# Where the row statistics, the bias load and the last MLP product stand in a kernel of linear attention and MLP

## The chip, the cores and the metric

The kernel runs on one core of a Trainium2 chip. The metric is device time in microseconds of one execution, as the median of several runs. A profile describes one execution of the same kernel. TensorE is written PE (its weight loads PEld), VectorE DVE, ScalarE ACT, GpSimd POOL, SyncE SP.

## What is computed

For 2048 tokens of width 512, a layer norm feeds two branches that are added to the input: a linear attention with 32 heads of 16 (feature map: softmax of a projection and of its negative), and an MLP of width 1792 with the mish activation.

```python
def _A_ref(x, wqkv, w_phi, wo):
    # q, k, v: (x @ wqkv) split into 32 heads of 16
    pq = jnp.einsum("bhsd,hdf->bhsf", q, w_phi)
    pk = jnp.einsum("bhsd,hdf->bhsf", k, w_phi)
    phi_q = jnp.concatenate([_softmax(pq, axis=-1), _softmax(-pq, axis=-1)], axis=-1)
    phi_k = jnp.concatenate([_softmax(pk, axis=-1), _softmax(-pk, axis=-1)], axis=-1)
    kv = jnp.einsum("bhsf,bhsd->bhfd", phi_k, v)
    z  = jnp.einsum("bhsf->bhf", phi_k)
    num = jnp.einsum("bhqf,bhfd->bhqd", phi_q, kv)
    den = jnp.einsum("bhqf,bhf->bhq", phi_q, z)[..., None] + 1e-6
    o = num / den
    return (o, heads joined) @ wo

def _B_ref(x, w1, b1, w2):
    h = jnp.einsum("bsd,df->bsf", x, w1) + b1
    sp = jnp.log1p(jnp.exp(-jnp.abs(h))) + jnp.where(h > 0, h, jnp.zeros_like(h))
    act = h * jnp.tanh(sp)
    return jnp.einsum("bsf,fd->bsd", act, w2)

x = A_x
xn = _layernorm(x, axis=-1)
return x + _A_ref(xn, A_wqkv, A_w_phi, A_wo) + _B_ref(xn, B_w1, B_b1, B_w2)
```

## The kernel before

The tokens are worked on in four groups (NG) of 512, each of four tiles (TPG) of 128 rows. At the start all weights are loaded, w_phi is folded into the q and k weights (wqp, wkp), and the mean and the reciprocal deviation of every row are worked out: those of group 0 from one load, those of the other 12 tiles from a second one. A framework puts each engine's instructions in an order of its own, by priority and dependence, and derives the waits; a line's place in the text is not its place in the queue.

```python
xs_v = x2.rearrange("(g t p) d -> p (g t) d", t=TPG, p=P)
x_stats0 = prep_w.tile([P, TPG, D], BF16, name="x_stats0")
nc.sync.dma_start(x_stats0[:], xs_v[:, 0:TPG, :])
wqk = prep_w.tile([P, KT, 2 * D], BF16, name="wqk")
nc.scalar.dma_start(wqk[:], wqkv_v[:, :, 0 : 2 * D])
# ... (cut): w_phi on ACT, wv on SP, w1 on ACT, wo on SP, w2 on ACT
b1b = wts.tile([P, FT], BF16, name="b1b")
with nc.allow_non_contiguous_dma(reason="tiny bias load"):
    nc.scalar.dma_start(b1b[:], b1_v[:, :])
b1f = wts.tile([P, FT], FP32, name="b1f")
nc.vector.tensor_copy(b1f[:], b1b[:])
# ... (cut): tiles that live throughout
stats0 = prep_w.tile([P, TPG, nc.vector.BN_STATS_DIM], FP32, name="stats0")
for tt in range(TPG):
    nc.vector.bn_stats(stats0[:, tt, :], x_stats0[:, tt, :])
for tt in range(TPG):
    nc.vector.bn_aggr(mv[:, tt, :], stats0[:, tt, :])
nc.scalar.activation(rstd[:, 0:TPG], mv[:, 0:TPG, 1], ACT.Sqrt, bias=eps_t[:])
nc.vector.reciprocal(rstd[:, 0:TPG], rstd[:, 0:TPG])

def finish_ln_stats():
    statpool = tc.alloc_tile_pool(name="statpool", bufs=1)
    x_stats = statpool.tile([P, NT - TPG, D], BF16, name="x_stats")
    nc.sync.dma_start(x_stats[:], xs_v[:, TPG:NT, :])
    stats = statpool.tile([P, NT, nc.vector.BN_STATS_DIM], FP32, name="stats")
    for tt in range(TPG, NT):
        nc.vector.bn_stats(stats[:, tt, :], x_stats[:, tt - TPG, :])
    for tt in range(TPG, NT):
        nc.vector.bn_aggr(mv[:, tt, :], stats[:, tt, :])
    nc.scalar.activation(rstd[:, TPG:NT], mv[:, TPG:NT, 1], ACT.Sqrt, bias=eps_t[:])
    nc.vector.reciprocal(rstd[:, TPG:NT], rstd[:, TPG:NT])
    statpool.release()
# ... (cut): masks, and Wbd, the block diagonal of w_phi
    for mi, base_col in ((0, 0), (1, D)):
        pfs = [
            ps_fold.tile([P, D], FP32, name=f"pfold{mi}_{kt}", tag="fold")
            for kt in range(KT)
        ]
        for j in range(4):
            ptr = ps_prep.tile([P, D], BF16, name="ptrw", tag="prep")
            for kt in range(KT):
                nc.tensor.transpose(
                    ptr[:, kt * P : (kt + 1) * P],
                    wqk[:, kt, base_col + j * P : base_col + (j + 1) * P],
                    ident[:],
                )
            wT = tmp.tile([P, D], BF16, name="wT")
            nc.scalar.copy(wT[:], ptr[:])
            for kt in range(KT):
                nc.tensor.matmul(
                    pfs[kt][:, j * P : (j + 1) * P],
                    lhsT=wT[:, kt * P : (kt + 1) * P],
                    rhs=Wbd[:, j, :],
                    start=True,
                    stop=True,
                )
        dst = wqp if mi == 0 else wkp
        for kt in range(KT):
            nc.vector.tensor_copy(dst[:, kt, :], pfs[kt][:])
prep_w.release()
```

Pass A, for each group: normalise and transpose x, project to v, k and q, take both exponentials (stage_front); softmax sums and scaling (stage_phi); transposes of phi(q) and the sums over tokens kvacc (stage_kq); the first MLP product with exp (stage_h); ln and tanh over all 1792 units (stage_lt); the second MLP product (stage_mb), which runs one group late.

```python
# ... (cut): pools of pass A; PSUM: tr 1, kq 1 (two banks), mm 2, kv 1, oB 2
def stage_front(g):
    xg = xpool.tile([P, TPG, D], BF16, name="xg")
    nc.sync.dma_start(xg[:], x_g[g])
    # ... (cut): xn <- (xg - mean) * rstd, four tiles on DVE; xnT <- transposes of xn; for four tiles: pv -> vext, ppkq -> e1, e2 (exp of it and of its negative)

def stage_h(st):
    uu = mpool.tile([P, FT, 512], BF16, name="uu")
    for f in range(FT):
        ph = ps_mm.tile([P, 512], FP32, name="pmm", tag="mm")
        for kt in range(KT):
            nc.tensor.matmul(
                ph[:],
                lhsT=w1_sb[:, kt, f * P : (f + 1) * P],
                rhs=xnT[:, kt, :],
                start=(kt == 0),
                stop=(kt == KT - 1),
            )
        nc.scalar.activation(
            uu[:, f, :], ph[:], ACT.Exp, bias=b1f[:, f : f + 1]
        )
    return uu

def stage_lt(uu):
    th = mpool.tile([P, FT, 512], BF16, name="th", bufs=1)
    nc.scalar.activation(th[:], uu[:], ACT.Ln, bias=1.0)
    nc.scalar.activation(uu[:], uu[:], ACT.Ln)
    nc.scalar.activation(th[:], th[:], ACT.Tanh)
    return (uu, th)

def stage_mb(st, lt):
    lnu, th = lt
    acts = []
    for f in range(FT):
        a = apool.tile([P, 512], BF16, name="act")
        nc.vector.tensor_tensor(
            out=a[:], in0=lnu[:, f, :], in1=th[:, f, :], op=ALU.mult
        )
        acts.append(a)
    pobs = []
    for t in range(TPG):
        poB = ps_oB.tile([P, 512], FP32, name="poB", tag="oB")
        for f in range(FT):
            nc.tensor.matmul(
                poB[:],
                lhsT=acts[f][:, t * P : (t + 1) * P],
                rhs=w2_sb[:, f, :],
                start=(f == 0),
                stop=(f == FT - 1),
            )
        tt = g * TPG + t
        nc.vector.tensor_copy(xb_all[:, tt, :], poB[:])
    return pobs

st = [None] * NG
lt = [None] * NG
st[0] = stage_front(0)
finish_ln_stats()
for g in range(NG):
    uu = stage_h(st[g])
    if g > 0:
        stage_mb(st[g - 1], lt[g - 1])
    lt[g] = stage_lt(uu)
    stage_phi(st[g])
    stage_kq(st[g])
    if g + 1 < NG:
        st[g + 1] = stage_front(g + 1)
nc.vector.tensor_tensor(
    out=kvm[:],
    in0=kvacc[:],
    in1=KVmask[:, None, :].to_broadcast([P, 8, 136]),
    op=ALU.mult,
)
stage_mb(st[NG - 1], lt[NG - 1])
```

Pass B needs the sums over all tokens (kvm), so it runs after the last group: numerator and denominator from phi(q) (pnd), the quotient o_t, its transpose oT, then the output projection poA, started with an identity product that adds x, and the MLP result xb_all added at the end.

```python
# ... (cut): pools of pass B: o_t 5, oT 2, rdt 4, yg 2, xg2 2; PSUM: pnd 4, ptr2 2, poA 2

xbpool = p2.enter_context(tc.tile_pool(name="pb_x", bufs=2))
for g in range(NG):
    gs = slice(g * 512, (g + 1) * 512)
    xg2 = xbpool.tile([P, TPG, D], BF16, name="xg2")
    nc.scalar.dma_start(xg2[:], x_g[g])

    o_tiles = []
    for t in range(TPG):
        tok0 = g * 512 + t * P
        o_t = opool.tile([P, 512], BF16, name="o_t")
        for j in range(4):
            pnd = ps_w.tile([P, 136], FP32, name="pnd", tag="pnd")
            for pl in range(2):
                s = 2 * j + pl
                nc.tensor.matmul(
                    pnd[:],
                    lhsT=phiqT_all[:, s, tok0 : tok0 + P],
                    rhs=kvm[:, s, :],
                    start=(pl == 0),
                    stop=(pl == 1),
                )
            rdt = rpool.tile([P, 8], FP32, name="rdt")
            nc.vector.reciprocal(rdt[:], pnd[:, 128:136])
            nc.vector.tensor_tensor(
                out=o_t[:, j * P : (j + 1) * P].rearrange(
                    "p (h e) -> p h e", e=16
                ),
                in0=pnd[:, 0:128].rearrange("p (h e) -> p h e", e=16),
                in1=rdt[:, :, None].to_broadcast([P, 8, 16]),
                op=ALU.mult,
            )
        o_tiles.append(o_t)
    oT = oTpool.tile([P, 4, 512], BF16, name="oT")
    for j in range(4):
        ptr = ps_tr2.tile([P, 512], BF16, name="ptr2", tag="tr2")
        for t in range(TPG):
            nc.tensor.transpose(
                ptr[:, t * P : (t + 1) * P],
                o_tiles[t][:, j * P : (j + 1) * P],
                ident[:],
            )
        nc.scalar.copy(oT[:, j, :], ptr[:])

    yg = ypool.tile([P, TPG, D], BF16, name="yg")
    for t in range(TPG):
        tt = g * TPG + t
        poA = ps_oA.tile([P, 512], FP32, name="poA", tag="oA")
        nc.tensor.matmul(
            poA[:],
            lhsT=ident[:],
            rhs=xg2[:, t, :],
            start=True,
            stop=False,
        )
        for j in range(4):
            nc.tensor.matmul(
                poA[:],
                lhsT=oT[:, j, t * P : (t + 1) * P],
                rhs=wo_sb[:, j, :],
                start=False,
                stop=(j == 3),
            )
        nc.vector.tensor_tensor(
            out=yg[:, t, :], in0=poA[:], in1=xb_all[:, tt, :], op=ALU.add
        )
    nc.sync.dma_start(out_g[g], yg[:])
```

The softmax here doesn't subtract the row's maximum and nothing guards it: scores larger than these inputs give would overflow.

## Time and profile before

| what | value |
|---|---|
| time, median of 4 runs | 283.81 us (282.29 to 284.76) |
| span of the profiled run | 282.3 us, 3341 instructions |
| PE busy | 215.8 us (76%), 1277 matmuls |
| DVE busy | 198.0 us (70%), 504 instructions |
| ACT busy | 167.0 us (59%), 136 instructions |
| POOL busy | 2.1 us (1%) |
| DMA | 14.38 MB |

Busy time is the sum of the instructions of an engine. Matmuls overlap in the array, so a busy PE is not PE at its peak: one 128x512 matmul is listed with a mean of about 380 ns, and in a run of them one starts every 216 ns. The profile has, among others, a table of busy time by stretch of the span, groups of instructions by line and shape, a timeline, a list of who waited for whom, and a chain: from the last instruction back, at each step to what released it. In lines of the profile, L392 is line 392 of the kernel before; names such as `poB` are those of the tiles, and `out<-in` gives what an instruction writes and reads. Group 0 to 3 are the token groups.

### The profile page before, as it was taken

How to read it: one execution, taken by the hardware profiler on the slowest of the kernel's cores; microseconds unless marked ns; L12 is line 12 of the kernel's file. 1: busy time of each engine (PE TensorE's matmuls, PEld its weight loads, DVE VectorE, ACT ScalarE, POOL GpSimd, SP SyncE). 2: the span in 40 equal slices, each digit the busy share in tenths (PEclk: the TensorE clock that was granted, in tenths of full speed). 3: DMA queues.
4: the chain of work that ended last, by engine and by line, in shares of the span. 5: the costliest groups of instructions: out<-in, count | busy, mean ns of one | idle time of the engine just before them, and what ended most of it. 6: DMA issues, size and time to landing. Idle time of an engine off the chain costs nothing.

```text
span 282.3 us, 3341 instructions
## 1 busy us (share of the span) xinstructions
PE 215.8 (76%) x1277; PEld 109.1 (39%) x1298; DVE 198.0 (70%) x504; ACT 167.0 (59%) x136; POOL 2.1 (1%) x14
## 2 busy tenths in 40 slices
PE   1122238998784699986999996899997589889973
PEld 0122214443541244445444445444444434444531
DVE  0405954999762799836899946699965783788762
ACT  0040110777999587899887899868799900320330
POOL 2000000000000000000000000000000000000000
PEclk9999999999999599999999999999999979999998
DMA  6996022200002000000000000000000300043122
GB/s 229 371 354 163 0 74 78 74 0 0 2 0 74 0 1 2 1 0 2 0 0 0 2 0 0 2 0 1 0 2 0 130 21 0 0 152 112 39 74 74
DMA packets 14687, 14.38 MB, mean 51 GB/s; under 512 B 2640, under 2 KB 13648, under 8 KB 14672
## 3 DMA queue, kind: packets, MB, share of 16 engines
q1 hardware_dynamic: 7360, 7.34, 8.2%
q10 hardware_dynamic: 7312, 6.84, 7.6%
q8 instruction: 10, 0.16, 0.2%
q14 instruction: 5, 0.04, 0.0%
HBM read 12.08 MB, written 2.10 MB: 50 GB/s over the span
## 4 chain that ended last, share of the span: by engine, by line
PE 52%; ACT 18%; DVE 13%; DMA 8%; issue 7%; SPq 1%; ACTq 0%; DVEq 0%
PE poB L392 13%; PE pmm L359 13%; DMA x_stats<-in_A_x_dram 8%; PE ppkq L249 5%; PE ppkq L257 5%; PE poA L490 5%; ACT th L373 4%; ACT th L375 4%; PE pmm L237 4%; DVE stats L125 3%; ACT e L266 3%; DVE o_t L458 2%; DVE phiqT_all L330 2%; ACT e L267 2%; PE ptr L325 2%
## 5 line engine op out<-in xcount | busy, mean ns | idle before, releaser
L392 PE MATMUL poB<-w_sb,act 128*128 128x512 bf16 x218 | 52.0, 388 | 7.5 <-DVE act L384 7.1
L359 PE MATMUL pmm<-xnT,w_sb 128*128 128x512 bf16 x219 | 52.1, 378 | 1.1 <-ACT uu L366 0.8
L366 ACT ACTIVATE uu<-pmm,b1f 128x512 bf16<-128x512 f32 x56 | 37.2, 691 | 11.8 <-PE pmm L359 7.6
L392 PEld LDWEIGHTS <-act 128*128 128x128 bf16 x224 | 22.3, 100 | 35.1 <-DVE act L384 9.3
L359 PEld LDWEIGHTS <-w_sb 128*128 128x128 bf16 x224 | 21.8, 97 | 28.9 <-issue 4.7
L476 ACT COPY oT<-ptr 128x512 bf16<-128x512 bf16 x16 | 8.7, 588 | 39.3 <-PE ptr L471 22.5
L400 DVE CAST xb_all<-poB 128x512 bf16<-128x512 f32 x16 | 11.0, 690 | 21.1 <-PE poB L392 21.1
L384 DVE TENSOR_TENSOR act<-uu,th 128x512 bf16<-128x512 bf16 x56 | 19.6, 416 | 7.9 <-ACT th L375 7.9
L374 ACT ACTIVATE uu<-uu 128x7168 bf16<-128x7168 bf16 x4 | 24.7, 6177 | 0.1
L375 ACT ACTIVATE th<-th 128x7168 bf16<-128x7168 bf16 x4 | 24.7, 6177 | 0.0
L373 ACT ACTIVATE th<-uu 128x7168 bf16<-128x7168 bf16 x4 | 24.7, 6177 | 0.0
L266 ACT ACTIVATE e<-ppkq 128x1024 bf16<-128x1024 f32 x16 | 16.3, 1021 | 12.1 <-PE ppkq L257 12.0
L237 PE MATMUL pmm<-wv,xnT 128*128 128x512 bf16 x64 | 20.4, 400 | 0.2
L178 PE MATMUL pfold<-Wbd,wT 128*128 128x128 bf16 x32 | 4.9, 305 | 19.7 <-DVE wqp L187 10.6
L278 DVE TENSOR_REDUCE ss<-e 128x64 f32<-128x1024 bf16 x16 | 19.3, 1209 | 0.0
L284 DVE TENSOR_REDUCE ss<-e 128x64 f32<-128x1024 bf16 x16 | 19.3, 1206 | 0.0
L325 PE MATMUL ptr<-ident,e 128*128 128x128 bf16 x128 | 12.7, 217 | 8.3 <-DVE phiqT_all L330 8.2
L249 PE MATMUL ppkq<-wkp,xnT 128*128 128x512 bf16 x58 | 18.1, 403 | 1.2 <-ACT e L267 0.8
L330 DVE COPY phiqT_all<-ptr 128x512 bf16<-128x512 bf16 x32 | 13.6, 424 | 7.1 <-PE ptr L325 6.9
L257 PE MATMUL ppkq<-wqp,xnT 128*128 128x512 bf16 x64 | 17.3, 395 | 0.0
L497 DVE TENSOR_TENSOR yg<-poA,xb_all 128x512 bf16<-128x512 f32 x16 | 10.7, 689 | 8.9 <-PE poA L490 8.7
L449 PE MATMUL pnd<-kvm,phiqT_all 128*128 128x136 bf16 x128 | 14.1, 227 | 3.7 <-DVE kvm L416 1.9
(66 smaller groups left out, 289.4 us busy)
## 6 DMA issues: line engine op xcount, KB each, us to landing
w_sb<-in_B_w_dram ACTq DMA_DIRECT2D x2, 1792.0 KB, 18.8
xg<-in_A_x_dram SPq DMA_DIRECT2D x4, 512.0 KB, 3.5
xg<-in_A_x_dram ACTq DMA_DIRECT2D x4, 512.0 KB, 4.0
out_dram<-yg SPq DMA_DIRECT2D x4, 512.0 KB, 3.2
x_stats<-in_A_x_dram SPq DMA_DIRECT2D x1, 1536.0 KB, 21.8
wqk<-in_A_wqkv_dram ACTq DMA_DIRECT2D x1, 1024.0 KB, 7.6
x_stats<-in_A_x_dram SPq DMA_DIRECT2D x1, 512.0 KB, 6.1
wv<-in_A_wqkv_dram SPq DMA_DIRECT2D x1, 512.0 KB, 8.3
```

Source lines behind the costliest of these rows:

```text
L237: nc.tensor.matmul(pv[:], lhsT=xnT[:, kt, tok0 : tok0 + P], rhs=wv[:, kt, :], start=(kt == 0), stop=(kt == KT - 1),)
L249: nc.tensor.matmul(ppkq[:, 0, :], lhsT=xnT[:, kt, tok0 : tok0 + P], rhs=wkp[:, kt, :], start=(kt == 0), stop=(kt == KT - 1),)
L257: nc.tensor.matmul(ppkq[:, 1, :], lhsT=xnT[:, kt, tok0 : tok0 + P], rhs=wqp[:, kt, :], start=(kt == 0), stop=(kt == KT - 1),)
L266: nc.scalar.activation(e1[:], ppkq[:], ACT.Exp)
L278: nc.vector.reduce_sum(ss1[:], e1[:].rearrange("p s (h e) -> p s h e", e=16), axis=AX.X,)
L359: nc.tensor.matmul(ph[:], lhsT=w1_sb[:, kt, f * P : (f + 1) * P], rhs=xnT[:, kt, :], start=(kt == 0), stop=(kt == KT - 1),)
L366: nc.scalar.activation(uu[:, f, :], ph[:], ACT.Exp, bias=b1f[:, f : f + 1])
L373: nc.scalar.activation(th[:], uu[:], ACT.Ln, bias=1.0)
L374: nc.scalar.activation(uu[:], uu[:], ACT.Ln)
L375: nc.scalar.activation(th[:], th[:], ACT.Tanh)
L384: nc.vector.tensor_tensor(out=a[:], in0=lnu[:, f, :], in1=th[:, f, :], op=ALU.mult)
L392: nc.tensor.matmul(poB[:], lhsT=acts[f][:, t * P : (t + 1) * P], rhs=w2_sb[:, f, :], start=(f == 0), stop=(f == FT - 1),)
```

## The change

It changes four things. First, the rows of group 0 are loaded once, by POOL's queue, and both its statistics and its normalisation use that tile; the load kept apart for the statistics goes. Second, the statistics of the other 12 tiles, and the cast of the bias, are put behind the last vext copy of group 0 (`issue_after`), so that the weight folding and group 0 need not wait for them; the bias load moves from ACT's queue to SP's. Third, the pools of pass A are released one by one, so that those of pass B can be opened while the buffers of the MLP live on; the second MLP product of the last group is split into its element products (`mb_acts`) and its matmuls (`mb_mm`), and the matmuls may be put between the pieces of pass B. Fourth, in pass B the numerator tile holds two blocks, so that one reciprocal and one product serve both; PSUM buffers become 3 (pnd), 1 (transposes) and 2 (poA) beside 2 of the MLP; the quotient tiles have 8 buffers instead of 5, and x is loaded by POOL's queue.

```diff
@@ -80,8 +80,6 @@
 
     prep_w = tc.alloc_tile_pool(name="prep_w", bufs=1)
     xs_v = x2.rearrange("(g t p) d -> p (g t) d", t=TPG, p=P)
-    x_stats0 = prep_w.tile([P, TPG, D], BF16, name="x_stats0")
-    nc.sync.dma_start(x_stats0[:], xs_v[:, 0:TPG, :])
     wqk = prep_w.tile([P, KT, 2 * D], BF16, name="wqk")
     nc.scalar.dma_start(wqk[:], wqkv_v[:, :, 0 : 2 * D])
     Wsrc = prep_w.tile([P, 4, DH], BF16, name="Wsrc")
@@ -97,9 +95,8 @@
     nc.scalar.dma_start(w2_sb[:], w2_v[:, :, :])
     b1b = wts.tile([P, FT], BF16, name="b1b")
     with nc.allow_non_contiguous_dma(reason="tiny bias load"):
-        nc.scalar.dma_start(b1b[:], b1_v[:, :])
+        nc.sync.dma_start(b1b[:], b1_v[:, :])
     b1f = wts.tile([P, FT], FP32, name="b1f")
-    nc.vector.tensor_copy(b1f[:], b1b[:])
 
     phiqT_all = persist.tile([P, 8, S], BF16, name="phiqT_all")
     kvacc = persist.tile([P, 8, 136], FP32, name="kvacc")
@@ -107,14 +104,6 @@
     rstd = persist.tile([P, NT], FP32, name="rstd")
-    ... (cut: statistics of group 0, as printed above)
 
     def finish_ln_stats():
         statpool = tc.alloc_tile_pool(name="statpool", bufs=1)
@@ -187,24 +176,27 @@
                 nc.vector.tensor_copy(dst[:, kt, :], pfs[kt][:])
     prep_w.release()
 
-    with ExitStack() as p1:
-        ... (cut: pools as before)
-        def stage_front(g):
-            xg = xpool.tile([P, TPG, D], BF16, name="xg")
-            nc.sync.dma_start(xg[:], x_g[g])
+    if True:
+        mpool = tc.alloc_tile_pool(name="pa_mish", bufs=1)
+        apool = tc.alloc_tile_pool(name="pa_act", bufs=14)
+        ps_oB = tc.alloc_tile_pool(name="ps_oB", bufs=2, space=bass.MemoryType.PSUM)
+        ... (cut: the other pools of pass A, with their sizes as before, ps_kv last)
+
+        last_front = [None]
+
+        def stage_front(g, xg=None):
+            if xg is None:
+                xg = xpool.tile([P, TPG, D], BF16, name="xg")
+                nc.sync.dma_start(xg[:], x_g[g])
             xn = xnpool.tile([P, TPG, D], BF16, name="xn")
             for t in range(TPG):
                 tt = g * TPG + t
@@ -241,7 +233,7 @@
                         start=(kt == 0),
                         stop=(kt == KT - 1),
                     )
-                nc.vector.tensor_copy(
+                last_front[0] = nc.vector.tensor_copy(
                     vext[:, t, :, 0:128], pv[:].rearrange("p (j c) -> p j c", j=4)
                 )
                 ppkq = ps_kq.tile([P, 2, 512], FP32, name="ppkq", tag="pkq")
@@ -375,8 +367,7 @@
             nc.scalar.activation(th[:], th[:], ACT.Tanh)
             return (uu, th)
 
-        def stage_mb(st, lt):
-            g, xg, xnT, vext, e1_tiles, e2_tiles = st
+        def mb_acts(st, lt):
             lnu, th = lt
             acts = []
             for f in range(FT):
@@ -385,6 +376,10 @@
                     out=a[:], in0=lnu[:, f, :], in1=th[:, f, :], op=ALU.mult
                 )
                 acts.append(a)
+            return acts
+
+        def mb_mm(st, acts):
+            g = st[0]
             ...
@@ -400,10 +395,113 @@
                 nc.vector.tensor_copy(xb_all[:, tt, :], poB[:])
             return pobs
 
+        def stage_mb(st, lt):
+            return mb_mm(st, mb_acts(st, lt))
+
+        def alloc_passB_pools():
+            pb = {}
+            pb["x"] = tc.alloc_tile_pool(name="pb_x", bufs=2)
+            pb["ot"] = tc.alloc_tile_pool(name="pb_ot", bufs=8)
+            pb["oT"] = tc.alloc_tile_pool(name="pb_oT", bufs=2)
+            pb["r"] = tc.alloc_tile_pool(name="pb_r", bufs=4)
+            pb["y"] = tc.alloc_tile_pool(name="pb_y", bufs=2)
+            pb["ps_w"] = tc.alloc_tile_pool(name="pb_ps_w", bufs=3, space=bass.MemoryType.PSUM)
+            pb["ps_tr2"] = tc.alloc_tile_pool(name="pb_ps_tr", bufs=1, space=bass.MemoryType.PSUM)
+            pb["ps_oA"] = tc.alloc_tile_pool(name="pb_ps_oA", bufs=2, space=bass.MemoryType.PSUM)
+            return pb
+
+        def passB_attn(pb, g):
+            tok_base = g * 512
+            xg2 = pb["x"].tile([P, TPG, D], BF16, name="xg2")
+            nc.gpsimd.dma_start(xg2[:], x_g[g])
+            # ... (cut: loop over tiles, as before)
+                for jj in range(2):
+                    pnd = pb["ps_w"].tile([P, 2, 136], FP32, name="pnd", tag="pnd")
+                    for jl in range(2):
+                        for pl in range(2):
+                            s_ = 2 * (2 * jj + jl) + pl
+                            nc.tensor.matmul(
+                                pnd[:, jl, :],
+                                lhsT=phiqT_all[:, s_, tok0 : tok0 + P],
+                                rhs=kvm[:, s_, :],
+                                start=(pl == 0),
+                                stop=(pl == 1),
+                            )
+                    rdt = pb["r"].tile([P, 2, 8], FP32, name="rdt")
+                    nc.vector.reciprocal(rdt[:], pnd[:, :, 128:136])
+                    nc.vector.tensor_tensor(
+                        out=o_t[:, jj * 2 * P : (jj + 1) * 2 * P].rearrange(
+                            "p (j h e) -> p j h e", j=2, e=16
+                        ),
+                        in0=pnd[:, :, 0:128].rearrange("p j (h e) -> p j h e", e=16),
+                        in1=rdt[:, :, :, None].to_broadcast([P, 2, 8, 16]),
+                        op=ALU.mult,
+                    )
+                o_tiles.append(o_t)
+            # ... (cut: transposes and copies to oT, as before)
+            return xg2, oT
+
+        def passB_out(pb, g, xg2, oT):
+            # ... (cut: poA, yg and store, as before)
+
+        def emit_passB(pb, g):
+            passB_out(pb, g, *passB_attn(pb, g))
+
         st = [None] * NG
         lt = [None] * NG
-        st[0] = stage_front(0)
-        finish_ln_stats()
+        xg0 = xpool.tile([P, TPG, D], BF16, name="xg")
+        nc.gpsimd.dma_start(xg0[:], x_g[0])
+        stats0 = spool.tile([P, TPG, nc.vector.BN_STATS_DIM], FP32, name="stats0")
+        for tt in range(TPG):
+            nc.vector.bn_stats(stats0[:, tt, :], xg0[:, tt, :])
+        for tt in range(TPG):
+            nc.vector.bn_aggr(mv[:, tt, :], stats0[:, tt, :])
+        nc.scalar.activation(
+            rstd[:, 0:TPG], mv[:, 0:TPG, 1], ACT.Sqrt, bias=eps_t[:]
+        )
+        nc.vector.reciprocal(rstd[:, 0:TPG], rstd[:, 0:TPG])
+        st[0] = stage_front(0, xg=xg0)
+        with tc.issue_after(last_front[0].ins):
+            nc.vector.tensor_copy(b1f[:], b1b[:])
+            finish_ln_stats()
         for g in range(NG):
             uu = stage_h(st[g])
             if g > 0:
@@ -413,91 +511,25 @@
             stage_kq(st[g])
             if g + 1 < NG:
                 st[g + 1] = stage_front(g + 1)
+        for pool in (ps_kv, ps_mm, ps_kq, ps_tr, vpool, epool, spool, xnTpool, xnpool, xpool):
+            pool.release()
         nc.vector.tensor_tensor(
             out=kvm[:],
             in0=kvacc[:],
             in1=KVmask[:, None, :].to_broadcast([P, 8, 136]),
             op=ALU.mult,
         )
-        stage_mb(st[NG - 1], lt[NG - 1])
-
-    with ExitStack() as p2:
-        ... (cut: pass B as printed above)
+        pb = alloc_passB_pools()
+        acts3 = mb_acts(st[NG - 1], lt[NG - 1])
+        for g in range(NG - 1):
+            emit_passB(pb, g)
+        att3 = passB_attn(pb, NG - 1)
+        mb_mm(st[NG - 1], acts3)
+        passB_out(pb, NG - 1, *att3)
+        release_passB_pools(pb)
+        ps_oB.release()
+        apool.release()
+        mpool.release()
```

## The prediction

> **What bounds the kernel now.** I read the busy slices first: no engine leads throughout (PE 76%, DVE 70%, ACT 59%), so the span has to be cut into stages. The table of busy time by stretch does it (columns: stretch, its length, busy us of PE, weight load, DVE, ACT, POOL, granted clock, DMA share, GB/s):
>
> ```profile
> 0.00:24.20 24.20, 5.81 (x42) 4.38 (x42) 3.62 (x12) 3.61 (x6) 1.64 (x12) 1.00 0.96 322
> 24.20:43.00 18.80, 4.30 (x28) 2.82 (x29) 14.90 (x40) 2.34 (x5) 0.00 (x0) 1.00 0.16 33
> ...
> 226.00:240.00 14.00, 13.21 (x61) 6.06 (x62) 8.20 (x26) 0.00 (x0) 0.00 (x0) 0.90 0.02 6
> 240.00:282.30 42.30, 32.83 (x249) 17.17 (x249) 29.25 (x129) 8.72 (x16) 0.00 (x0) 0.97 0.23 75
> ```
>
> For 43 us TensorE does almost nothing, and in the last 42 us no engine is full. The middle (43 to 226) is nearly full on PE or ACT. The change touches the two ends, so I then read the chain that ended last at both. The beginning (start, length, what):
>
> ```profile
> 2.38 21.82 DMA x_stats<-in_A_x_dram
> 24.23 6.03 DVE stats L125 x10
> 30.41 1.17 DVE stats L125 x2
> 31.58 0.82 DVE mv L127 x12
> 32.98 2.34 DVE wqp L187 x4
> ...
> 37.47 3.89 issue
> 42.68 0.44 DVE xnT L228
> ```
>
> The load of 12 row tiles for the statistics, landed at 24.2, and their 12 sums stand in VectorE's queue ahead of the copies that free the fold's PSUM banks (L187). The folded weights, and with them everything, wait for statistics that only groups 1 to 3 need. The 3.89 us of "issue" is the reload of group 0's x, issued at 37.49, when memory came free. The timeline shows a second hold:
>
> ```profile
> 8.43 8.21 ACTq L100 DMA_DIRECT2D b1b<-in_B_b_dram  x1
> 16.72 1.28 ACT L116 ACT_TABLE_LOAD   x1 [16.72 <-issue]
> 18.22 1.05 ACT L176 COPY wT<-ptrw 128x512 bf16<-128x512 bf16 x2
> ```
>
> ACT's queue spends 8.21 us issuing the 3.5 KB bias load, so the first fold copy (L176), whose transposes were done at about 9, starts at 18.2. At the other end:
>
> ```profile
> 225.98 4.78 DVE L384 TENSOR_TENSOR act<-uu,th 128x512 bf16<-128x512 bf16 x14 [0.35 <-ACT th L375]
> 226.87 13.02 PE L392 MATMUL poB<-w_sb,act 128*128 128x512 bf16 x54 [0.74 <-DVE act L384]
> 242.65 2.13 ACT L476 COPY oT<-ptr 128x512 bf16<-128x512 bf16 x4 [16.70 <-DVE rdt L457]
> ```
>
> The 56 matmuls of the last group's second MLP product run alone from 226.9 to 239.9, then pass B (attention output) runs from 240 to 282: four groups, whose last yg adds start at 248.5, 258.2, 267.9 and 277.6, about 9.6 apart.
>
> **What the Trainium skill says.** "DMA: Bandwidth & Descriptors", section "Queues, rings and completion order", has each DMA engine go round the queues packet by packet; so a third queue beside two busy ones should get about a third. The trace has only two: 14.4 MB on two hardware queues, 322 GB/s while both were full. The same page's "Anatomy of one DMA" gives 2.0 us plus bytes over 436 GB/s for a load issued by GpSimd, an estimated 3.2 us for 512 KB alone; no GpSimd load is in this trace, the same size from SP took 3.5. "SBUF — State Buffer", section "SBUF: two separate sides", warns that such a load can be held up while VectorE runs in a two-port mode; nothing here shows it yet. "ScalarE: Activation LUTs", section "What ACT_TABLE_LOAD costs", gives about 1283 ns; the trace agrees (1283 ns).
>
> **The change, the beginning.** Group 0's statistics now come from the tile of group 0 itself (loaded by GpSimd's queue), the 12 other tiles' statistics move in VectorE's queue behind group 0's four vext copies, and the bias load moves to SP. Step by step, on the clock of the profile:
> 1. wqk. The first 1 MB on ACT's queue landed at 8.4 beside one other queue. With a third I estimate 10, and Wsrc, 10.1 before, at 11.7. Group 0's x, issued at about 1.7 (where POOL's memset of eps ends), with the page's fixed 2.0 us and 4.6 us for 512 KB at a third of 330 GB/s, is an estimated 8.5; I take 9 to 10, as three queues may not share evenly.
> 2. VectorE: Wbd to 12.1, then four stats (2.47 before), four aggregates (0.36): 15.0. ACT: table load 1.28 and root 0.30: 16.6. Reciprocal and four xn (1.38): 18.2.
> 3. ACT in its queue: fold copies 1 and 2 at 11 to 12, the root until 16.6, then the others. First fold done at about 18.3 (before, 4.0 us from the first copy with nothing between).
> 4. Four wqp copies at 18.3. Before, from the first wqp copy at 32.98 to the last wkp copy at 39.65 was 6.7 us; I keep 6.9, so 25.2. xn is long transposed, so the first xnT copy starts at about 25.2 instead of 42.68: **17.4 us gained**, the reload of x included.
> 5. What is given back. In group 0 VectorE now has 12 stats, 12 aggregates and the bias cast (7.3 + 0.9 + 0.2 = 8.4 us) before the softmax sums. Before, it stood idle 6.9 us at 93.5 waiting for the first tanh, so about 1.5 us comes through. ACT gets the root of 12 columns with two table loads (2 x 1.28 + 0.30 = 2.9 us) between exponentials. It was partly waiting for TensorE there (0.8 us a tile), and its first exp table load, 1.28 us after the wait for PE, now waits only for VectorE and can be done ahead; net +1.0, beside the 1.5 and not on top. Cost: **1.5 us**.
>    The 1.5 MB load of statistics must land before about 34; with 7.6 MB in all at 322 GB/s it should be there by about 25.
>
> Sum at the beginning: 17.4 - 1.5 = 15.9.
>
> **The change, the end.** poB of group 3 is put between the pieces of pass B, the numerator and its reciprocal go two blocks at a time (32 of each instead of 64), and the PSUM buffers change from 4, 2, 2 to 3 (pnd), 1 (transpose), 2 (poA).
> 1. TensorE's pure work from 226 on, by the chain's spacing of 0.216 us for a 512-column matmul: 136 (56 poB, 80 poA) is 29.4; 128 pnd at 0.06 is 7.7; 64 transposes at 0.06 is 3.8. Together 40.9, against 50.7 from 226.87 to the end of the last poA at 277.55. So at most some 10 us can go.
> 2. VectorE for each group: before, eight steps of 0.635 (2 reciprocals, 2 products) and four yg of 0.69: 5.1 + 2.8 = 7.9. After, four steps. A product of twice the columns gains 128 columns at 1.04 ns (from 690 ns for 512 columns against 286 for 128): 0.42; a reciprocal of 16 instead of 8 columns, at 7.8 ns a column (540 against 295 ns for 64 and 32), 0.24. A step is about 1.0 with overlap: 4.0 + 2.8 = 6.8. Saved 1.1 a group.
> 3. By the built order, TensorE does 20 pnd before the first poB, then 21 poB paced by the 14 act products (ready at 230.8), then alternates. Followed by hand, group 0's output is done at about 242.9 instead of 249.2, with 30 of 56 poB behind it. A group then takes about 8.5 (before 9.6, less 1.1): groups 1 and 2 end at 251.4 and 259.9. In group 3 the transposes alternate with the last 19 poB (4 a step against a copy of 0.59) and 20 poA follow: about 10.8, at 270.7. Last yg and output store, as before, 4.7: 275.4. **7 us gained.**
>
> Sum: 283.8 - 15.9 - 7 = **260.9, say 261**.
>
> **Rivals.** (a) The loads at the start become the bound: the third queue delays wqk, or the GpSimd load comes late. For it: DMA busy 0.96 until 24.2. Against: all that the fold and group 0's first products need is 2.0 MB of 7.6. If x lands at 14 instead of 9.5 the gain shrinks by 2; at 20, by 8, giving 269. (b) The moved statistics return on ACT and VectorE in group 0. If the root holds ACT the full 2.9 and VectorE's 8.4 come through beside the 6.9 of slack only in part, 4 more are lost: 265. (c) The single transpose buffer makes each of 16 transpose sets wait for a copy of 0.59 on ACT. Filled by two poA and four pnd (0.67), which is about even; if it isn't, the tail gains only 2 to 3: 265. (d) TensorE runs the tail without gaps: the tail gains 10, and 258. Slower than before would need both ends to fail: there is no step that adds more than 3 us to the path.
>
> **Range and chances.** The beginning may give 11 to 18, the tail 3 to 10; both at their ends at once is unlikely. 255 to 268 should hold it 8 times in 10. Below 278.1 (2%) it falls in nearly all of these: faster 0.96, same 0.03, slower 0.01.
>
> **What would show each step.** Right: the first xnT copy at 24 to 27; no wait of VectorE for the 12-tile load on the chain; the first act product about 52 us after that first xnT copy (50.8 before); poB mixed with pnd; from the first act product to the end 49 to 50 us instead of 56.3. Wrong: an xn or stats instruction waiting for the GpSimd load beyond 14; ACT idle before the second root; waits of transposes on the oT copy adding up to over 3 us; groups still 9.6 apart. If the beginning gains under 10 or the tail nothing, the working above is wrong at that step, even if the sum fits.

## The result, and the profile after

The changed kernel takes 258.5 us (median of 10, 257.0 to 259.2) against 283.9 (15 runs) before: a ratio of 0.911, 95% interval 0.909 to 0.913. The prediction was 261.0.

The table of busy time by stage cuts both kernels at the same events: the first xnT copy, then the first Mish product of each group, then the end (columns as in the prediction's first fence). The tail before:

```profile
225.98:282.30 56.32, 46.06 (x306) 23.23 (x310) 37.46 (x154) 8.72 (x16) 0.00 (x0) 0.95 0.18 58
```

After:

```profile
25.15:78.91 53.76, 41.76 (x216) 21.72 (x220) 42.95 (x97) 41.71 (x32) 0.20 (x1) 0.85 0.07 23
78.91:122.82 43.91, 40.32 (x234) 20.04 (x237) 36.21 (x78) 37.99 (x28) 0.21 (x1) 1.00 0.04 13
122.82:165.78 42.96, 39.53 (x229) 19.64 (x232) 34.30 (x73) 37.20 (x27) 0.78 (x2) 1.00 0.00 1
165.78:210.31 44.53, 39.83 (x233) 19.74 (x234) 36.84 (x77) 37.93 (x27) 0.74 (x1) 1.00 0.08 24
210.31:256.80 46.49, 40.87 (x299) 22.54 (x305) 33.16 (x92) 9.38 (x16) 1.50 (x2) 0.99 0.20 69
```

The last group's first product comes at 210.31 instead of 225.98: 15.67 us from the beginning. The tail is 46.5 instead of 56.3: 9.8 us. In the tail VectorE's work fell by 4.3 us. TensorE's fell by 5.2 with the same matmuls: one that stands alone is counted with 0.38 us, one that is followed at once with 0.216.

The timeline of the beginning (start, length, engine, line):

```profile
1.70 0.88 POOL L491 DMA_DIRECT2D xg<-in_A_x_dram  x1
2.37 10.15 SPq L111 DMA_DIRECT2D x_stats<-in_A_x_dram  x1
10.55 1.07 ACT L165 COPY wT<-ptrw 128x512 bf16<-128x512 bf16 x2 [3.28 <-PE ptrw L159]
15.91 1.05 ACT L165 COPY wT<-ptrw 128x512 bf16<-128x512 bf16 x2
17.54 2.48 DVE L176 CAST wqp<-pfold 128x512 bf16<-128x512 f32 x4
25.15 0.42 DVE L220 COPY xnT<-ptr 128x512 bf16<-128x512 bf16 x1 [0.67 <-PE ptr L215]
```

The first fold copy starts at 10.55 instead of 18.2. The bias load's hold has not gone: on SP it is the load behind it whose issue takes 10.15 us, but nothing urgent stands there. One hold is left: the second pair of fold copies starts at 15.91, behind the root of group 0 on ACT (table load 14.41, root 15.70), though its transposes were done at 13.6. What the chain begins with is a load of 16 KB, the source of Wbd, ahead of Wbd and group 0's statistics in VectorE's order:

```profile
1.32 9.82 DMA Wsrc<-in_A_w_phi_dram
11.24 0.42 DVE Wbd L142
11.66 2.38 DVE stats L494 x4
```

In the tail, first what TensorE waited for (its whole answer: engine, line, releaser, total, times, longest), then the end of the chain:

```profile
PE poB L387 <- DVE act L375: 0.7, 1, 0.7
```

```profile
244.10 0.25 PE ptr L452 x4
244.35 0.86 PE poB L387 x4
245.21 0.22 PE ptr L452 x4
245.43 0.86 PE poB L387 x4
...
252.17 0.69 DVE yg L480
```

From 236 on the chain is matmul after matmul up to the last yg, with poB matmuls between the transposes; between 230.4 and 234.5 it still runs over VectorE. The listed waits alone don't show the gain: they are 0.7 us in 46.5, but in the kernel before only 3.1 in 56.3. The stretch from the first poB to the end of the last poA does. It was 50.7 us (226.87 to 277.55) and is 41.4 (210.79 to 252.15). From the chains, the last poA of the kernel before, then the first poB and the last poA of the kernel after:

```profile
276.67 0.88 PE poA L490 x4
277.57 0.69 DVE yg L497
```

```profile
210.79 4.96 PE poB L387 x21
...
251.27 0.88 PE poA L473 x4
252.17 0.69 DVE yg L480
```

The granted clock in the tail was 0.95 before (0.76 in its first 6 us) and 0.99 after. The 56 poB took 13.0 us before, against 56 x 0.216 = 12.1, so an estimated 0.9 of the 9.8 us, in the poB, may be the clock's.

### The profile page after: what moved, and what is told of

It reads as the page before. It is cut to its first block, busy times and chain, and to the rows that moved or that the text cites. A ratio compares the mean times of both kernels' runs of the same rounds, so it can differ in the third digit from the quotient of the medians.

```text
span 256.8 us, 3284 instructions
## 1 busy us (share of the span) xinstructions
PE 211.2 (82%) x1276; PEld 110.8 (43%) x1298; DVE 193.5 (75%) x440; ACT 171.9 (67%) x139; POOL 5.9 (2%) x19
## 4 chain that ended last, share of the span: by engine, by line
PE 58%; DVE 20%; ACT 11%; issue 5%; DMA 4%; ACTq 0%; DVEq 0%
PE poB L387 13%; PE pmm L351 12%; PE pmm L229 7%; PE poA L473 5%; PE ppkq L241 5%; PE ppkq L249 4%; DMA Wsrc<-in_A_w_phi_dram 4%; DVE phiqT_all L322 4%; PE ptr L317 4%; DVE stats L114 3%; PE ptr L215 2%; ACT th L365 2%; ACT th L367 2%; PE pnd L430 2%; PE ptr L452 2%
## 5 line engine op out<-in xcount | busy, mean ns | idle before, releaser
L387 PEld LDWEIGHTS <-act 128*128 128x128 bf16 x224 | 21.0, 98 | 25.5 <-DVE act L375 3.9
L457 ACT COPY oT<-ptr 128x512 bf16<-128x512 bf16 x16 | 9.4, 586 | 27.5 <-PE ptr L452 27.5
L229 PE MATMUL pmm<-wv,xnT 128*128 128x512 bf16 x64 | 21.7, 419 | 0.6 <-issue 0.4
L317 PE MATMUL ptr<-ident,e 128*128 128x128 bf16 x128 | 13.9, 232 | 9.3 <-DVE phiqT_all L322 7.7
L241 PE MATMUL ppkq<-wkp,xnT 128*128 128x512 bf16 x58 | 17.5, 391 | 1.9 <-ACT e L259 1.5
L328 PE MATMUL pkv<-vext,e 128*128 128x136 bf16 x128 | 14.5, 239 | 4.6 <-DVE e L289 4.6
L473 PE MATMUL poA<-wo_sb,oT 128*128 128x512 bf16 x61 | 17.1, 380 | 0.1
L317 PEld LDWEIGHTS <-e 128*128 128x128 bf16 x128 | 10.6, 103 | 14.4 <-issue 11.7
L249 PE MATMUL ppkq<-wqp,xnT 128*128 128x512 bf16 x64 | 16.4, 379 | 0.0
```

The source lines that it names most:

```text
L229: nc.tensor.matmul(pv[:], lhsT=xnT[:, kt, tok0 : tok0 + P], rhs=wv[:, kt, :], start=(kt == 0), stop=(kt == KT - 1),)
L241: nc.tensor.matmul(ppkq[:, 0, :], lhsT=xnT[:, kt, tok0 : tok0 + P], rhs=wkp[:, kt, :], start=(kt == 0), stop=(kt == KT - 1),)
L249: nc.tensor.matmul(ppkq[:, 1, :], lhsT=xnT[:, kt, tok0 : tok0 + P], rhs=wqp[:, kt, :], start=(kt == 0), stop=(kt == KT - 1),)
L317: nc.tensor.transpose(ptr[:, t * P : (t + 1) * P], planes[pl][t][:, 1, j * P : (j + 1) * P], ident[:],)
L387: nc.tensor.matmul(poB[:], lhsT=acts[f][:, t * P : (t + 1) * P], rhs=w2_sb[:, f, :], start=(f == 0), stop=(f == FT - 1),)
L473: nc.tensor.matmul(poA[:], lhsT=oT[:, j, t * P : (t + 1) * P], rhs=wo_sb[:, j, :], start=False, stop=(j == 3),)
```

## The experiments

Ratios are to the kernel before, run beside each; brackets are 95% intervals. "First copy" is the first xnT copy, "tail" the time from the last group's first Mish product to the end.

**start_only**: the kernel before with the beginning of the change alone, its pools in their old order.

```diff
-    x_stats0 = prep_w.tile(...); nc.sync.dma_start(x_stats0[:], ...)
-        nc.scalar.dma_start(b1b[:], b1_v[:, :])
+        nc.sync.dma_start(b1b[:], b1_v[:, :])
+        nc.gpsimd.dma_start(xg0[:], x_g[0])        # stats of group 0 from xg0
+        with tc.issue_after(last_front[0].ins):
+            nc.vector.tensor_copy(b1f[:], b1b[:])
+            finish_ln_stats()
```

> Only the beginning is changed (rows of group 0 loaded once, other statistics behind group 0, bias on SP's queue); pass B and the last MLP product stay as before. Theory: the two ends do not touch each other, so the 15.7 us by which the changed kernel reaches the first act product of the last group sooner come out whole: 268.1 us (267 to 269.5), first xnT copy at about 25, tail from the first act product to the end 56.3. Rival: part of the gain is lost again or was owed to the tail's new buffers, and the time is above 270.

Measured: 274.7 us, 0.968 [0.964, 0.972]. The gain is 9.5 and not 16. One of its four runs, the profiled one, was slowed throughout (370.8 us) and is left out of the median, and only order and waits at its start are read. The timeline of POOL, with the wait in brackets:

```profile
18.13 0.88 POOL L398 DMA_DIRECT2D xg<-in_A_x_dram  x1 [15.85 <-PE pfold L167]
```

The load of x waited 15.85 us for the fold's last use of its memory. In the old order of pools the x tile lies where the fold's weights were released. The change opens the MLP pools first, so that x lies elsewhere. That line looked like bookkeeping for the tail.

**start_pools**: the same with the MLP's SBUF pools opened first.

```diff
     with ExitStack() as p1:
+        mpool = p1.enter_context(tc.tile_pool(name="pa_mish", bufs=1))
+        apool = p1.enter_context(tc.tile_pool(name="pa_act", bufs=14))
         xpool = p1.enter_context(tc.tile_pool(name="pa_x", bufs=1))
         ...
-        mpool = ...
-        apool = ...
```

> As start_only (beginning changed, pass B and the last MLP product as before), but with the two MLP pools opened ahead of the pools of x, as in the changed kernel, so that the tile of group 0's x lies where no folding weight lies. Theory: in start_only that load waited for the folding weights' memory (it was issued at 18.1 us instead of 1.7), and this alone kept back 7 us; now the first xnT copy stands at about 25 and the time is 268.1 us (267 to 269.5). Rival: the 7 us were lost elsewhere, and the time stays at 274 to 276.

Measured: 271.7 us, 0.958 [0.951, 0.964], between the two. The first copy is at 24.46 and the last group's first product at 209.60, so the beginning has its full gain, 16.4. But the tail is 60.5 us instead of 56.3. The load of x for pass B, on ACT's queue, first in the kernel before and then here:

```profile
222.01 0.94 ACTq L439 DMA_DIRECT2D xg<-in_A_x_dram  x2
```

```profile
224.74 0.93 ACTq L444 DMA_DIRECT2D xg<-in_A_x_dram  x2
```

Before, it was issued 4.0 us ahead of the last group's first product; here it is 15.1 us behind it, when the products of the MLP are used up, and the chain passes through it. Not all of the 4.2 us are the load's. The copy of the last poB starts 15.1 us after the first product instead of 13.9, so 1.2 us were lost ahead of the load's effect, while the granted clock was 0.65 (first 7.4 us; before, 0.76 in the first 6). So the two halves of the change share the pools: the order that frees x at the beginning delays x at the end, unless pass A's pools are released apart from the MLP's, as the change does (its loads for pass B are issued at 165.0).

**tail_only**: the kernel before with the change's pools, pass B and mixing, and the old beginning.

```diff
+        pb = alloc_passB_pools()
+        acts3 = mb_acts(st[NG - 1], lt[NG - 1])
+        for g in range(NG - 1): emit_passB(pb, g)
+        ...                                        # beginning as before
```

> Only the end is changed (last MLP product mixed into pass B, two blocks for each numerator tile, other PSUM buffers); the beginning stays as before. Theory: the tail takes 46.5 us instead of 56.3, so 274.1 us (273 to 275.5). Rival, the prediction's own sum for the tail: 7 us, 277 us.

Measured: 273.7 us, 0.964 [0.961, 0.967]; its tail is 46.7 us (225.96 to 272.7). The tail's gain stands by itself: 9.6 us by the profile, 10.5 by the times, not 7.

**no_mix**: the kernel after with all poB matmuls ahead of pass B.

```diff
-        acts3 = mb_acts(st[NG - 1], lt[NG - 1])
+        stage_mb(st[NG - 1], lt[NG - 1])
-        mb_mm(st[NG - 1], acts3)
```

> The changed kernel, but the matmuls of the last group's MLP product are all written ahead of pass B, as before the change. Theory: TensorE's gaps in pass B are no longer filled by them, so the tail grows by 4 to 7 us, to 262.5 to 265.5. Rival: with two blocks a tile pass B has no gaps left to fill, and the time rises by less than 2 us.

Measured: 265.0 us, 0.933 [0.929, 0.936]: mixing is worth 6.5 us. The tail is 53.1. The group of TensorE's transposes in the tail (idle time ahead of it in the last column):

```profile
L452 PE MATMUL ptr<-ident,o_t 128*128 128x128 bf16 x63 | 7.3, 218 | 2.6 <-ACT oT L457 2.6
```

They wait 2.6 us for the copies that free the single transpose buffer; in the kernel after the same group waits 0.1. Rival (c) of the prediction is real where nothing fills the wait, and mixing hides it.

**one_block** and **split_ops**: the numerator one block to a tile (three banks hold three blocks instead of six, 64 reciprocals and 64 products instead of 32 each); and two blocks to a tile as in the kernel after, but with 64 and 64 operations.

```diff
-                for jj in range(2):
-                    pnd = pb["ps_w"].tile([P, 2, 136], FP32, ...)
+                for j in range(4):
+                    pnd = pb["ps_w"].tile([P, 136], FP32, ...)   # one_block
```

```diff
-                    nc.vector.reciprocal(rdt[:], pnd[:, :, 128:136])
+                    for jl in range(2):                           # split_ops
+                        nc.vector.reciprocal(rdt[:], pnd[:, jl, 128:136])
```

> The changed kernel, but each numerator tile holds one block again (64 reciprocals and 64 products instead of 32 and 32), still three PSUM buffers. VectorE gets about 9 us more in the tail (64 x (178 + 286) ns less 32 x (243 + 411) ns). Theory: TensorE paces the tail and VectorE has 13 us free there, so the time rises by 1 to 4 us, to 259.5 to 262.5. Rival: pairing the blocks is what took VectorE off the path, and nearly all of the 9 us comes back: 266 or more.

> The changed kernel with its numerator tiles of two blocks, and so six blocks in flight, but with a reciprocal and a product for each block again (64 and 64 instead of 32 and 32). It parts the two things that one_block changed together. Theory: VectorE's 9 us more are what cost 9 us there, so this is 266 to 267.5 too. Rival: with three banks of one block each TensorE waited for banks; then this one stays at 259 to 262.

Measured: one_block 267.5 us, 0.941 [0.937, 0.944]; split_ops 264.1, 0.932 [0.928, 0.937]. split_ops lies between its two expectations. Of the 9 us that one_block loses, the number of operations is 5.6, and the depth of the buffers with what else differs the other 3.4 (one_block's granted clock in the tail was 0.94, split_ops's 1.00). The groups of VectorE in the tail, after and then split_ops (mean ns of one behind the busy time; then idle before):

```profile
L439 DVE TENSOR_TENSOR o_t<-pnd,rdt 128x256 bf16<-128x256 f32 x30 | 11.7, 412 | 0.2
L480 DVE TENSOR_TENSOR yg<-poA,xb_all 128x512 bf16<-128x512 f32 x16 | 10.7, 686 | 2.3 <-PE poA L473 2.0
```

```profile
L441 DVE TENSOR_TENSOR o_t<-pnd,rdt 128x128 bf16<-128x128 f32 x61 | 15.2, 280 | 0.2
L482 DVE TENSOR_TENSOR yg<-poA,xb_all 128x512 bf16<-128x512 f32 x16 | 10.7, 689 | 7.7 <-PE poA L475 7.4
```

A product of half the width costs 280 ns and not 206, a reciprocal of half the columns 187 instead of 242. VectorE has 4.7 us more to do, TensorE gets its inputs later, and the waits of yg for poA grow from 2.0 to 7.4. one_block's group 0 is also 1.0 us later, which this doesn't explain.

**bias_act**: the bias load back on ACT's queue.

```diff
-        nc.sync.dma_start(b1b[:], b1_v[:, :])
+        nc.scalar.dma_start(b1b[:], b1_v[:, :])
```

> The changed kernel with the bias load back on ACT's queue, behind w2. Theory: ACT's queue is held about 8 us by it, from 6 to 14, so the first fold copy starts at about 15.5 instead of 10.55; the root of group 0 comes 2 to 3 us later and the time is 260.5 to 262. Rival: the load no longer holds ACT, or the hold is covered by the wait for wqk and the statistics: 258 to 259.

Measured: 264.4 us, 0.933 [0.928, 0.938], 5.9 more than the kernel after and more than expected. The timeline of ACT:

```profile
6.08 12.01 ACTq L98 DMA_DIRECT2D b1b<-in_B_b_dram  x1
18.12 1.28 ACT L165 ACT_TABLE_LOAD   x1 [18.12 <-issue]
19.42 1.07 ACT L165 COPY wT<-ptrw 128x512 bf16<-128x512 bf16 x2
```

Beside three queues the issue of 3.5 KB holds ACT for 12.01 us (8.21 before the change). The first fold copy is 8.87 us later, the first xnT copy (31.31) 6.16 later, and 5.2 of it reaches the last group. This one line of the change is worth over a third of the gain at the beginning.

**stats_early**: the later tiles' statistics no longer tied behind group 0's last vext copy.

```diff
         with tc.issue_after(last_front[0].ins):
             nc.vector.tensor_copy(b1f[:], b1b[:])
-            finish_ln_stats()
+        finish_ln_stats()
```

> The changed kernel, but the statistics of the 12 other tiles are no longer tied behind group 0's last vext copy (the bias cast still is). They then stand in VectorE's queue ahead of xn and of the wqp copies. Theory: the copies wait for the 12-tile load (at about 26) and 7 us of sums, so the first xnT copy comes at about 41 instead of 25, and the 3 us given back in group 0 are not paid: 270 to 273 us. Rival: the load and the other moves make most of the gain at the beginning, and this costs under 5: below 263.5.

Measured: 271.4 us, 0.957 [0.951, 0.964]. The first copy is at 40.53 instead of 25.15. 15.4 us are lost there and 12.8 reach the last group: 2.6 are saved in between, where group 0 now carries neither the statistics nor the two table loads.

**no_table**: the root of the twelve later tiles left out, with an exponential in its place, so that ACT needs no other table there. It is meant to show what the two table loads cost.

```diff
-        nc.scalar.activation(rstd[:, TPG:NT], mv[:, TPG:NT, 1], ACT.Sqrt, bias=eps_t[:])
+        nc.scalar.activation(rstd[:, TPG:NT], mv[:, TPG:NT, 1], ACT.Exp, bias=eps_t[:])
```

> The kernel after with Exp in place of Sqrt for the twelve later tiles, so that ScalarE keeps the table it has loaded: the two table loads at 43.43 and 45.05 us (1.28 us each) go, all else stays. Theory (the 3.0 us that group 0 gives back are VectorE's, its 8.4 us of statistics, and the table loads lie beside them): 257.8 to 258.8 us, the first Mish product of group 0 at most 0.7 us earlier than 78.9. Rival (the table loads stand in the path of the exponentials, as much as the statistics): 256.0 to 257.3 us, the first product 1.3 to 2.6 us earlier.

Measured: 258.6 us, 0.912 [0.907, 0.916]: no change. The first tanh of groups 0 and 1 on ACT, after and then no_table:

```profile
58.81 6.18 ACT L365 ACTIVATE th<-uu 128x7168 bf16<-128x7168 bf16 x1
...
102.44 6.18 ACT L365 ACTIVATE th<-uu 128x7168 bf16<-128x7168 bf16 x1
```

```profile
55.58 6.18 ACT L365 ACTIVATE th<-uu 128x7168 bf16<-128x7168 bf16 x1
...
102.51 6.18 ACT L365 ACTIVATE th<-uu 128x7168 bf16<-128x7168 bf16 x1
```

Without the loads ACT is 3.2 us earlier in group 0, and the first product 1.4 earlier, as the rival had it. By group 1's tanh nothing of it is left, so the first Mish product is a poor mark of group 0's progress; group 1's first tanh is a better one. The time agrees with the theory, but it doesn't decide between the two. In groups 1 to 3 of this program an eviction of the MLP has moved (see root_pool), and its last tanh comes 2.0 us later than in the kernel after (206.12 against 204.10), which can hide a gain of that size. What the two table loads cost is not shown.

**by_group**: no second load of x. The statistics of groups 1 to 3 come from each group's own tile, and their root from three Newton steps on POOL.

```diff
-            finish_ln_stats()
+            if g + 1 < NG:
+                with tc.issue_after(last_front[0].ins):
+                    xg_next = load_stats(g + 1)    # load, stats, root on POOL
```

> The kernel after without the second load of x: the statistics of groups 1 to 3 are taken from each group's own tile, behind the last vext copy of the group before, and their root by three Newton steps on GpSimd, so that neither 12 tiles of statistics nor two table loads fall into group 0. Theory (the statistics in group 0 cost the 3.0 us because VectorE is the engine that group 0 waits for; later groups wait for TensorE and can carry 2.8 us each): group 0's first Mish product 50.5 to 51.5 us after the first xnT copy instead of 53.8, the time 255.0 to 257.0 us. Rival (every group waits for VectorE as group 0 does, the cost comes back in three parts): 257.5 to 259.5 us.

Measured: 256.6 us, 0.906 [0.901, 0.910], which its interval doesn't tell from the kernel after. Group 0 took 51.4 us to its first product, as the theory said, but group 1's tanh comes 77.4 us after the first copy, as in the kernel after (77.3), and groups 1 to 3 take 134.5 instead of 131.4. In the profile the cost comes back, as the rival had it. But the profiled run was the slowest of the four (258.7 us), and in its group 2 both evictions of the place discussed under root_pool have moved, so it is not shown that the statistics are what costs there.

**all_pool**: by_group, with group 0's root on POOL too, and xn(0) behind the last wqp copy.

```diff
-        nc.scalar.activation(rstd[:, 0:TPG], mv[:, 0:TPG, 1], ACT.Sqrt, bias=eps_t[:])
-        nc.vector.reciprocal(rstd[:, 0:TPG], rstd[:, 0:TPG])
+        root_on_pool(0)
+            with tc.issue_after(wqp_last.ins):     # around xn(g)
```

> As by_group, and group 0's root on GpSimd too, with xn(0) behind the last copy of the first folded weight: the third wT copy then no longer waits on ScalarE behind the statistics, the table load and the root (in the kernel after the ptrw transposes were done at 13.6 and the second pair of copies began at 15.91). Theory (the root on ScalarE's queue holds the fold by 2.7 us): first xnT copy at 22.0 to 23.0 us instead of 25.15, the time 252.0 to 254.5 us. Rival (the fold is held by VectorE's statistics, 11.58 to 14.3, and by its copies in either case): first xnT copy at 24.3 or later, the time 254.5 to 257.0 us.

Measured: 253.2 us, 0.893 [0.890, 0.896], faster than the kernel after by 5.3. The timeline of its beginning:

```profile
13.30 1.07 ACT L152 COPY wT<-ptrw 128x512 bf16<-128x512 bf16 x2 [1.83 <-PE ptrw L146]
...
22.72 0.42 DVE L240 COPY xnT<-ptr 128x512 bf16<-128x512 bf16 x1 [0.55 <-PE ptr L235]
```

The third fold copy starts at 13.30 instead of 15.91, and the first xnT copy 2.4 us earlier. The root on POOL takes 3.9 us (14.46 to 18.37), beside the fold. By group 1's tanh (97.11 against 102.44) the lead is 5.3 us; where the 2.9 beyond the first copy come from is not shown.

**root_pool**: the kernel after with both roots on POOL and xn(0) behind wqp; the twelve tiles' statistics stay in one block.

```diff
-        nc.scalar.activation(rstd[:, TPG:NT], mv[:, TPG:NT, 1], ACT.Sqrt, bias=eps_t[:])
-        nc.vector.reciprocal(rstd[:, TPG:NT], rstd[:, TPG:NT])
+        root_on_pool(statpool, slice(TPG, NT), NT - TPG)
```

> The kernel after with nothing changed but the root: both roots by three Newton steps on GpSimd, and xn(0) behind the last copy of the first folded weight; the twelve later tiles' statistics stay in one block in group 0, from their own load. It takes all_pool apart. Theory (what all_pool gained, 5.3 us against 258.5, comes from the fold that no longer waits for ScalarE's root, 2.4 us of the first xnT copy, and from the table loads off group 0, and where the statistics stand is worth little, as by_group's 2 us at most say): first xnT copy at 22.5 to 23.0 us, first Mish product of group 0 52 to 54 us behind it, the time 253.5 to 256.0 us. Rival (all_pool needed the statistics spread over the groups as well, because they and the 8.4 us of VectorE then in group 0 follow the earlier start): first xnT copy as early, but the time 256.5 to 258.5 us.

Measured: 256.6 us, 0.904 [0.901, 0.908]: the rival's time, but not by the rival's cause. The first copy is at 23.0 and group 1's tanh 75.5 us after it, 1.8 better than in the kernel after, though the statistics still stand in group 0. Then groups 2 and 3 take 45.0 each from tanh to tanh, where the kernel after took 43.4 and 44.6: 2.0 us lost. The MLP's evictions on ACT in group 2, after and then root_pool:

```profile
128.91 1.27 ACT L358 ACTIVATE uu<-pmm,b1f 128x512 bf16<-128x512 f32 x2 [0.86 <-DVE act L375]
```

```profile
125.12 0.69 ACT L381 ACTIVATE uu<-pmm,b1f 128x512 bf16<-128x512 f32 x1 [0.43 <-DVE act L398]
```

In this place between the exponentials two evictions stand in one program and one in the other. The missing one is made at the end of the group, where they come 0.9 us apart; for two groups that is 1.8 of the 2.0. The order that the framework built for groups 2 and 3 changed with an edit in group 0. no_table shows one eviction there too, and the same 45.0 twice. That the order is the cause is read from the timelines; it wasn't tried by itself.

## Why the prediction was right, and where it was not

**The beginning**, its steps 1 to 4. Group 0's x landed at 10.7 (9 to 10 predicted; the three terms given for it add to 8.3 and not 8.5, and nothing rests on that), the first fold copy came at 10.55 ("11 to 12"), the first wqp copy at 17.54 (18.3), the first xnT copy at 25.15 (25.2). The Trainium skill's "DMA: Bandwidth & Descriptors", "Queues, rings and completion order", agrees as far as seen: beside a third queue wqk took 9.1 us to landing instead of 7.6. The wait named in "SBUF — State Buffer", "SBUF: two separate sides", couldn't show in this load: its issue (1.70 to 2.58) was over before VectorE's first instruction, at 3.76. The wqp and wkp copies took the 6.9 us counted (17.54 to 24.47). But xn was not "long transposed": it was ready at 17.6, and its transposes waited for the wkp copies and came at 24.53, which put 0.7 us on the path. That made up for a fold 0.8 us earlier than predicted, so the 25.2 was met in part by luck. What the prediction hadn't seen is that this step needs the new order of pools, without which some 6 of its 16 us go (start_only).

**Step 5, what is given back.** The prediction's 1.5 us is 1.8 by group 1's first tanh: 77.3 us after the first xnT copy, against 75.5 before (118.16 - 42.68). Its reason fits the chain of the kernel after, in which the statistics of the 12 tiles stand (8.3 us of VectorE with the cast, where 8.4 were counted) and the table loads don't:

```profile
34.24 0.69 DVE vext L236
35.01 7.12 DVE stats L114 x12
42.13 0.80 DVE mv L116 x12
42.94 1.10 DVE ss L270
```

But no run isolates it. By the same mark no_table, without the table loads, gained nothing (77.3), and by_group, without the loads and with the statistics spread out, nothing either (77.4); root_pool gained 1.8 with the statistics in place, and stats_early 2.6 without either. These programs differ in order too, and in the granted clock of group 0 (0.80 to 0.98; kernel after 0.85, before 0.99). How the 1.8 us divide between statistics, table loads and clock stays open. The sign that the prediction named, the first Mish product 52 us after the first copy, failed (53.8, 3.0 more than before, of which 1.2 are made up by group 1's tanh). The sum of the beginning is 15.7 against 15.9. Rival (b), with 4 us more lost, is refuted as to its size.

**The tail, step 1**: the 40.9 us of pure work, a few pnd of it done ahead, stand against 41.4 from the first poB to the end of the last poA. That TensorE's busy time in the stage is 40.87 is a coincidence: it counts lone matmuls longer, and 299 of the 328 are recorded. **Step 2**: VectorE saved 1.08 a group (4.3 in all) against 1.1, with 412 and 242 ns for the two operations where 420 and 240 were estimated. **Step 3** failed, and is the whole error of the sum: the order followed by hand gave 49.4 and the tail took 46.5. From the last group's first product to the last yg it had 16.9, 8.5, 8.5 and 10.8 for the four groups and then 4.7; measured are 16.1, 7.8, 9.5, 8.5 and 4.6 (marks: the end of each group's last yg, for the fourth group its start). The mis-sized term is the waiting left between the matmuls: groups 0 and 1 came 1.5 us sooner than followed by hand, groups 2 and 3 together 1.3, the last one alone 2.3, as all its pnd had been done in group 2's stretch. The prediction had four poB a step (0.86 us) against a copy of 0.59, and the chain shows just that; but by its own spacings the 19 poB, 16 transposes and 20 poA of the last group are 9.4 us and not 10.8, and they took 9.35 (242.80 to 252.15). Rival (d), TensorE without gaps, which the prediction put at 258, is what happened: the 41.4 us show it, in tail_only the tail is 46.7 again, and without the mixing it is 53.1 (no_mix).

**Rivals (a) and (c).** Neither wqk nor x came late: the fold began at 10.55. A load does stand first on the chain, but it is the small Wsrc, landed at 11.1 where 11.7 was counted. The single transpose buffer costs 2.6 us without mixing and nothing with it.

## What to carry to other kernels

In a tail that TensorE could fill, first add up its pure work: if matmuls of another stage can be put between the steps that wait, expect a time near that sum, as here (41.4 us for 40.9), and check a schedule followed by hand against it. When a load is moved early, ask on whose released memory its tile lies; the order in which pools are opened can undo the move, at either end. And an edit at the beginning can change the order that is built for everything behind it, so a gain there has to be read again at later marks before its cause is named.

## What the runs showed of the hardware beyond this

The 3.5 KB bias load holds the queue that issues it: 8.21 us on ACT before, 12.01 in bias_act, and on SP 10.15, there shown by the issue of the load behind it (0.50 in bias_act, where the bias isn't on that queue). A 512 KB load issued by POOL took 0.75 to 0.88 us to issue and 4.2 us to land (median of five; 9.0 for the first, beside two full queues), against 3.6 from SP (median of three; 10.1 for the first, behind the load of the statistics). The granted clock in group 0 was 0.85 where it had been 0.99 before; no_table's group 0 was shorter at 0.80, so the clock alone doesn't set the time there; why it was lower stays open.
